# An attention state stored without its zero blocks, with the head pairs of odd batches swapped in PSUM

## The chip, the cores and the metric

The kernel runs on one core of a Trainium2 chip. The metric is the time of one execution on the device, in microseconds (us); lower is better.

## What is computed

A linear attention with a decaying state, then two feed-forward parts. The attention has 4 batches, 8 heads, 768 positions and head size 48:

```python
for t in range(S):
    cur = np.einsum('bhd,bhe->bhde', u[None] * kt, vt)
    y[:, :, t] = np.einsum('bhd,bhde->bhe', rt, state + cur)
    state = w[None, :, :, None] * state + np.einsum('bhd,bhe->bhde', kt, vt)
```

`y`, laid out as 3072 tokens by 384, goes into a soft mixture of experts (softmax of `x @ phi` over the tokens and over 32 slots, 8 experts with a hidden layer of 1024), and its result through a dense layer 384 to 2048 to 384 with a leaky ReLU. All of it is in fp32.

## The kernel before

The attention runs in chunks of 128 positions (`C`), 6 chunks of 4 head pairs: 24 **units**, unit `i` being chunk `c = i // 4` and pair `hp = i % 4`. A unit holds all 4 batches of its two heads. Head 0 of a pair lies on partitions 0 to 47, head 1 on 64 to 111; so a tile "of a pair" has 112 partitions (`R`).

For each unit TensorE (PE) runs these steps, in program order, with the names that the profile shows:

- `scores(i + 1)`: `A`, k against r, eight products of 48 rows, the two heads in two row tiles of the array, each head into a PSUM bank of its own.
- `attend(i)`: `y`, in two parts. The **state step** (line 392, from chunk 1 on): four products, one for each batch, `Sbd` (112 x 112, two 48 x 48 blocks on the diagonal and zeros elsewhere) against r. The **base step** (line 399): eight products of the masked scores `base` with v, the heads in two column tiles.
- `update(i)`: `U`, k against v for the next state, eight products of 48 columns.
- `logits(i - 1)`: `l`, `x @ phi`, four products of 32 weight columns, each batch in a column tile of its own.
- `tokens(i - 1)`: `px`, four transposes.

In the second unit of each chunk (`k == 1`) there are besides: `soft2`, which transposes two tiles of the chunk before (`pt`, which ScalarE copies to `dl` and `call`), and `slots` (`pS`, four products of 384 columns, the batches in four column tiles).

Around them GpSimd (POOL) scales r and forms the bonus product two units ahead (`scale`, `bonus`, `keys`); VectorE (DVE) scales k, puts the masked scores into `base` (`keep`, line 369), reduces the bonus to `Dg` (line 323), folds `U` into the state (line 422, one instruction for each head) and narrows a weight in eight of the units (`low`); ScalarE (ACT) writes `base` from `Dg` (line 338, eight instructions), copies `y` to `xT` (line 432) and `px` to `xtok`, and takes the exponentials of the softmax (`d`, line 483). The engines run their instructions in program order; no scheduler reorders them (`manual_schedule`). The line of all loads is SP's: in each unit a weight of 768 KB, and the r, k (512 KB) and v, k, r tokens (576 KB) of the unit four ahead, whose buffers (five of them) are freed by PE's last read.

PSUM has 8 banks: `A` two, `y` one, `ylast` one (it shares the tag of the powers `ETp`), `l` one, and three that rotate (`psM`) among `U`, `px`, `pS`, `pt` and `low`. The last unit writes two `y` tiles, so that ACT can copy the first half while PE makes the second.

After the attention come the expert layers (`ph`, `po`) and, from about 163 us on, 96 steps of the dense layer (`h`, and line 1005, `o`).

Of the kernel before, what the change touches and what calls it, by code (L numbers as in the profile page):

```python
# [8 lines left out]
F32 = mybir.dt.float32  # L9
# [4 lines left out]
ALU = mybir.AluOpType  # L14
AX = mybir.AxisListType
PSUM = bass.MemoryType.PSUM

B, H, S, D = 4, 8, 768, 48
C = 128
# [98 lines left out]
def chunked(ctx, tc, rk, tok, wT, urep, phi, w1, w2, win, wout, outT, dbg=None, check=False):  # L118
# [10 lines left out]
    phi_sb = cp.tile([R, NP, NS], F32, name="phi_sb")  # L129
# [69 lines left out]
    psM = att.enter_context(tc.tile_pool(name="psM", bufs=3, space=PSUM))  # L199
# [59 lines left out]
    warm = psY.tile([128, 512], F32, name="warm", tag="y")  # L259
# [3 lines left out]
    def warmup(n):  # L263
        for k in range(n):
            nc.tensor.matmul(warm, zz[:, 0:128], zz, start=True, stop=True)
# [24 lines left out]
    def powers_t(hp):  # L290
# [8 lines left out]
    Sbd = ap.tile([R, NP, B, R], F32, name="Sbd")  # L299
    nc.scalar.copy(  # L300
        Sbd.rearrange("p a b c -> p (a b c)"), zz[:R, 0:1].broadcast_to([R, NP * B * R])
    )
# [72 lines left out]
    yps, xT, xtok, lps, lw = {}, {}, {}, {}, {}  # L375

    def attend(i):
        c, hp = divmod(i, NP)
        y = yps[i] = psY.tile([128, B, C], F32, name=f"y{i}", tag="y")
        if i == NU - 1:  # L380
            ylast = psE.tile([128, B, C], F32, name="ylast", tag="E")
            yps[i] = y, ylast
        for _ in range(FILL.get(i + 1, 0)):
            nc.tensor.matmul(
                y.rearrange("p b t -> p (b t)"), zz[:, 0:128], zz, start=True, stop=True
            )
        v = tk_t[i][:, 0]
        for bs in (range(B),) if i < NU - 1 else (range(B // 2), range(B // 2, B)):
            if bs[0]:
                y = ylast  # L390
# [5 lines left out]
            for b in bs:  # L396
                for h in range(2):
                    n = 64 if c == 0 and h == 0 else D
                    nc.tensor.matmul(  # L399
                        y[64 * h : 64 * h + n, b, :], v[:, b, D * h : D * h + n],  # L400
                        base[i][:, h, b, :], start=c == 0, stop=True, skip_group_check=True,
                    )

    def update(i):
        c, hp = divmod(i, NP)
        if c < NC - 1:
            v = tk_t[i][:, 0]
            u = psM.tile([128, B, D], F32, name=f"U{i}", tag="m")
            kk = tk_t[i][:, 1]
            for b in range(B):  # L410
                for h in range(2):
                    nc.tensor.matmul(  # L412
                        u[64 * h : 64 * h + D, b, :], kk[:, b, D * h : D * h + D],
                        v[:, b, D * h : D * h + D], start=True, stop=True,
                    )
            for h in range(2):
                p = slice(64 * h, 64 * h + D)
                st = Sbd[p, hp, :, p]
                if c == 0:
                    nc.vector.tensor_copy(st, u[p])  # L420
                else:
                    nc.vector.scalar_tensor_tensor(  # L422
                        st, st, W128[p, hp : hp + 1], u[p], op0=ALU.mult, op1=ALU.add
                    )

    def evac(i):
        x = xT[i] = bp.tile([R, B, C], F32, name=f"xT{i}", tag="xT")
        if i == NU - 1:
            nc.scalar.copy(x[:, 0:2], yps[i][0][0:R, 0:2])
            nc.vector.tensor_copy(x[:, 2:4], yps[i][1][0:R, 2:4])  # L430
        else:
            nc.scalar.copy(x, yps[i][0:R])

    def logits(i):
        c, hp = divmod(i, NP)
        if hp == 0:
            lw[c] = psL.tile([128, 4, C], F32, name=f"l{c}", tag="l")
            lps[c] = lw[c][:, 0]
        for b in range(B):
            nc.tensor.matmul(  # L440
                lps[c][32 * b : 32 * b + 32, :], phi_sb[:, hp, :], xT[i][:, b, :],
                start=hp == 0, stop=hp == NP - 1, skip_group_check=True,
            )
# [57 lines left out]
    def soft2(c):  # L501
        pt = psM.tile([128, 2, 128], F32, name=f"pt{c}", tag="m")
# [7 lines left out]
    def slots(c):  # L510
        pS = psM.tile([128, DM], F32, name=f"pS{c}", tag="m")
        for b in range(B):
            nc.tensor.matmul(
                pS[32 * b : 32 * b + 32, :], dTs[c][:, 32 * b : 32 * b + 32], xtok[c][:, b, :],
                start=True, stop=True,
            )
        return pS
# [47 lines left out]
    for i in range(NU):  # L565
# [76 lines left out]
    pz = psM.tile([128, 512], F32, name="pz", tag="m")  # L642
    pt = psM.tile([128, 2, 128], F32, name="ptl", tag="m")
# [14 lines left out]
    pS = slots(NC - 1)  # L658
# [449 lines left out]
def _layout(i):  # L1108
# [27 lines left out]
    a["phi"] = ph.reshape(NP, 128, NS)[:, :R].transpose(1, 0, 2)  # L1136
# [42 lines left out]
```

## Time and profile before

| | us |
|---|---|
| median of 3 runs | 394.1 (393.93 to 395.03) |
| the profiled execution | 393.61 |
| its span, first to last instruction | 391.8 |
| the attention, to the last `y` product | 123.9 |

The granted TensorE clock is 1.00 (2.4 GHz) through the attention and 0.998 over the span. In the rows below a matmul of fp32 counts as two instructions (`x16` is eight products). The end of a matmul is modelled, and matmuls overlap: how long a step holds PE is read from its start to the start of the next step, not from its length.

### The profile page before, as it was taken

How to read it: one execution, taken by the hardware profiler on the slowest of the kernel's cores; microseconds unless marked ns; L12 is line 12 of the kernel's file. 1: busy time of each engine (PE TensorE's matmuls, PEld its weight loads, DVE VectorE, ACT ScalarE, POOL GpSimd, SP SyncE). 2: the span in 40 equal slices, each digit the busy share in tenths (PEclk: the TensorE clock that was granted, in tenths of full speed). 3: DMA queues.
4: the chain of work that ended last, by engine and by line, in shares of the span. 5: the costliest groups of instructions: out<-in, count | busy, mean ns of one | idle time of the engine just before them, and what ended most of it. 6: DMA issues, size and time to landing. Idle time of an engine off the chain costs nothing.

```text
span 391.8 us, 8004 instructions
## 1 busy us (share of the span) xinstructions
PE 375.6 (96%) x2978; PEld 289.9 (74%) x2978; DVE 278.8 (71%) x483; ACT 236.3 (60%) x551; POOL 149.9 (38%) x150
## 2 busy tenths in 40 slices
PE   6897999999999999899999999999999999999994
PEld 3566888887866343788888878888888888888883
DVE  6789898898973736757677764677866776586762
ACT  4377787878784215566676548667655445545540
POOL 4798999988630401145523332555200000000000
PEclk9999999999999999999999999999999999999999
DMA  7999999999997799500022220000000120021202
GB/s 255 413 419 414 413 416 417 416 418 416 408 364 255 280 390 416 215 0 0 2 81 81 82 80 2 1 0 3 1 1 2 54 106 2 2 109 53 80 1 88
DMA packets 21088, 70.07 MB, mean 179 GB/s; under 512 B 2240, under 2 KB 7344, under 8 KB 20912
## 3 DMA queue, kind: packets, MB, share of 16 engines
q1 hardware_dynamic: 21040, 69.47, 45.4%
q8 instruction: 25, 0.41, 0.4%
q14 instruction: 23, 0.19, 0.2%
HBM read 64.74 MB, written 4.72 MB: 177 GB/s over the span
## 4 chain that ended last, share of the span: by engine, by line
PE 78%; DVE 8%; POOL 5%; issue 4%; ACT 3%; POOLq 0%; DVEq 0%; ACTq 0%
PE o L1005 50%; PE h L948 6%; PE po L783 3%; PE ph L740 3%; PE y L392 3%; PE A L361 3%; PE y L399 2%; DVE base L369 2%; ACT base L338 2%; POOL rkb L309 2%; PE px L448 1%; DVE Dg L323 1%; PE U L412 1%; DVE Sbd L422 1%; PE l L440 1%
## 5 line engine op out<-in xcount | busy, mean ns | idle before, releaser
L962 ACT CAST gh<-t 128x512 fp32r<-128x512 f32 x94 | 58.4, 622 | 69.6 <-DVE t L958 66.6
L958 DVE TENSOR_TENSOR t<-t,h 128x512 f32<-128x512 f32 (+1 forms) x97 | 65.7, 678 | 25.0 <-ACT t L954 24.2
L1005 PE MATMUL o<-gh,wol 128*128 128x512 f32 x279 | 80.1, 393 | 0.0
L1005 PE MATMUL o<-gh,woh 128*128 128x512 f32 x279 | 80.0, 393 | 0.0
L1005 PE MATMUL o<-gl,woh 128*128 128x512 f32 x279 | 79.7, 392 | 0.0
L967 DVE TENSOR_TENSOR gl<-t,gh 128x512 fp32r<-128x512 f32 x71 | 50.3, 709 | 40.6 <-ACT gh L962 39.9
L954 ACT ACTIVATE t<-h 128x512 f32<-128x512 f32 (+1 forms) x97 | 57.4, 593 | 12.3 <-PE h L948 11.2
L1005 PEld LDWEIGHTS o<-gl,woh 128*128 128x128 f32 x279 | 52.4, 188 | 11.8
L1005 PEld LDWEIGHTS o<-gh,woh 128*128 128x128 f32 x279 | 52.4, 188 | 11.8 <-DVE sum L1076 0.2
L1005 PEld LDWEIGHTS o<-gh,wol 128*128 128x128 f32 x279 | 52.2, 188 | 11.8 <-issue 0.4
L338 ACT ACTIVATE base<-anti,Dg 128x128 f32<-128x128 f32 x176 | 53.9, 391 | 8.8 <-DVE Dg L323 8.8
L967 POOL TENSOR_TENSOR gl<-t,gh 128x512 fp32r<-128x512 f32 x23 | 34.3, 1491 | 51.0 <-ACT gh L962 43.1
L948 PE MATMUL h<-cT,Gs 128*128 128x512 f32 (+1 forms) x97 | 37.4, 391 | 1.4 <-ACT Gs L916 1.4
L369 DVE COPY_PREDICATED base<-mask,A 128x512 f32<-128x512 int32 x48 | 33.7, 733 | 4.1 <-ACT base L338 3.0
L361 PE MATMUL A<-rkb 48*128 48x128 f32 x384 | 28.2, 286 | 3.0 <-DVE base L369 1.3
L361 PEld LDWEIGHTS A<-rkb 48*128 48x128 f32 x384 | 23.8, 189 | 8.4 <-POOL rkb L309 2.8
L309 POOL TENSOR_TENSOR rkb<-rkb,ETw 112x512 f32<-112x512 f32 x23 | 27.5, 1198 | 4.1 <-DMA rkb<-in_rk_dram 3.9
L399 PE MATMUL y<-base,tk 128*48 128x128 f32 (+1 forms) x376 | 25.5, 277 | 0.0
L315 POOL TENSOR_TENSOR tk<-tk,u_sb 128x384 f32<-128x384 f32 x22 | 22.5, 1022 | 4.4 <-DMA tk<-in_tok_dram 2.4
L318 POOL TENSOR_TENSOR tk<-tk 128x384 f32<-128x384 f32 x22 | 22.3, 1012 | 1.7
L850 POOL TENSOR_TENSOR wol<-wor,woh 128x384 fp32r<-128x384 f32 x8 | 9.5, 1198 | 33.6 <-ACT woh L849 33.6
L399 PEld LDWEIGHTS y<-base,tk 128*48 128x48 f32 (+1 forms) x376 | 19.5, 124 | 3.7 <-issue 0.8
(200 smaller groups left out, 499.4 us busy)
## 6 DMA issues: line engine op xcount, KB each, us to landing
w<-in_w_dram SPq DMA_DIRECT2D x24, 768.0 KB, 9.8
tk<-in_tok_dram SPq DMA_DIRECT2D x23, 576.0 KB, 8.1
rkb<-in_rk_dram SPq DMA_DIRECT2D x24, 512.0 KB, 8.4
wir<-in_win_dram SPq DMA_DIRECT2D x8, 768.0 KB, 12.9
out_dram<-sum SPq DMA_DIRECT2D x17, 256.0 KB, 2.0
wor<-in_wout_dram SPq DMA_DIRECT2D x4, 768.0 KB, 8.4
wir<-in_wout_dram SPq DMA_DIRECT2D x4, 768.0 KB, 4.2
w2t<-in_w_dram SPq DMA_DIRECT2D x4, 576.0 KB, 5.7
```

What stands on the lines that cost most here:

```text
L309: (nc.vector if x else eng).tensor_tensor(t, t, e, op=ALU.mult)
L315: eng.tensor_tensor(rr, rr, u_sb[:, hp : hp + 1, :].broadcast_to([128, B, 2 * D]), op=ALU.mult)
L338: nc.scalar.activation(base[i][:, h, b, :], anti, AF.Copy, scale=Dg[i][:, h * B + b : h * B + b + 1])
L361: nc.tensor.matmul(a[:, h, b, :], rk_t[i][p0 : p0 + D, 1, b, :], rk_t[i][p0 : p0 + D, 0, b, :], start=True, stop=True,)
L369: nc.vector.copy_predicated(base[i][:, :, 2 * j : 2 * j + 2, :], mask.unsqueeze(1).unsqueeze(1).broadcast_to([128, 2, 2, C]), a[:, :, 2 * ...
L399: nc.tensor.matmul(y[64 * h : 64 * h + n, b, :], v[:, b, D * h : D * h + n], base[i][:, h, b, :], start=c == 0, stop=True, skip_group_chec ...
L948: nc.tensor.matmul(t, Gs[f // 8][:, f % 8 * 128 : f % 8 * 128 + 128], cT[blk // 3][:, blk % 3 * TB + c.start : blk % 3 * TB + c.stop], sta ...
L954: nc.scalar.mul(tt[n][:, c], t, 0.01)
L958: nc.vector.tensor_tensor(tt[n][:, c], tt[n][:, c], h, op=ALU.max)
L962: nc.scalar.copy(gh[n][:, c], tt[n][:, c])
L967: eng.tensor_tensor(gl[n][:, c], tt[n][:, c], gh[n][:, c].bitcast(F32), op=ALU.subtract)
L1005: nc.tensor.matmul(os[m][:, c], w[j][:, k, m * 128 : (m + 1) * 128], g[n][:, c], start=k == 0 and w is woh and g is gh and c.start == 0, s ...
```

## The change

`Sbd` becomes `St`, 112 partitions by 48 columns for each batch and pair, without the zero blocks; the copy that zeroed `Sbd` at the start goes away. The state step becomes eight products of 48 x 48. `y` becomes one tile `Y` of two banks for all units: the batch's parity `r` chooses the bank, its half `j` the place in it, and a head of parity `r` goes to partitions `64 * (h ^ r)`, so that in odd batches the two heads change places. Four products in a row then use the four quarters of the array (64 x 64 each). The base step follows the same places.

What reads `y` follows too: `phi` comes with a second copy with heads swapped (112 KB in place of 56), `slots` takes two products of 192 columns in place of one of 384 for odd batches, and `evac` copies from two banks. The new state is folded in by one DVE instruction of 112 partitions in place of two of 48; since it reads all 112, `U` of head 0 takes 64 weight columns in place of 48.

`Y` takes two banks: so `psM` keeps two buffers in place of three, and `ylast` is gone. `pt` moves from `psM` into the bank of `l`, so `logits` of a new chunk can begin only when `dl` and `call` are copied; `slots` is moved ahead of `logits`.

```diff
-    psM = att.enter_context(tc.tile_pool(name="psM", bufs=3, space=PSUM))
+    psM = att.enter_context(tc.tile_pool(name="psM", bufs=2, space=PSUM))
...
+    Y = psY.tile([128, 2, 4, C], F32, name="Y", tag="y")
...
-            for b in bs if c else ():
+        for j in range(B // 2) if c else ():
+            for r in range(2):
+                b = 2 * j + r
+                for h in range(2):
+                    g, p = 64 * (h ^ r), slice(64 * h, 64 * h + D)
+                    nc.tensor.matmul(
+                        Y[g : g + D, r, j, :], St[p, hp, b, :], rk_t[i][p, 0, b, :],
+                        start=j == 0, stop=False, skip_group_check=True,
+                    )
+        for j, r in ((0, 0), (0, 1), (1, 0), (1, 1)) if i < NU - 1 else ((0, 0), (1, 0), (0, 1), (1, 1)):
+            b = 2 * j + r
+            for h in range(2):
+                g = 64 * (h ^ r)
                 nc.tensor.matmul(
-                    y[0:R, b, :], Sbd[:, hp, b, :], rk_t[i][:, 0, b, :], start=b == bs[0],
-                    stop=False, skip_group_check=True,
+                    Y[g : g + D, r, j, :], v[:, b, D * h : D * h + D], base[i][:, h, b, :],
+                    start=c == 0, stop=True, skip_group_check=True,
                 )
...
+                    n = D if h else 64
                     nc.tensor.matmul(
-                        u[64 * h : 64 * h + D, b, :], kk[:, b, D * h : D * h + D],
+                        u[64 * h : 64 * h + n, b, :], kk[:, b, D * h : D * h + n],
...
-            for h in range(2):
-                p = slice(64 * h, 64 * h + D)
-                st = Sbd[p, hp, :, p]
...
+            st = St[:, hp]
...
-        pt = psM.tile([128, 2, 128], F32, name=f"pt{c}", tag="m")
+        pt = lw[c][:, 1:3]
...
+            p, x = slice(32 * b, 32 * b + 32), xtok[c][:, b, :]
+            for h in range(2) if b % 2 else (None,):
+                nc.tensor.matmul(
+                    pS[p] if h is None else heads(pS[p])[:, h], dTs[c][:, p],
+                    x if h is None else heads(x)[:, 1 - h], start=True, stop=True,
+                )
...
-        if i >= 1:
-            logits(i - 1)
         if c and k == 1:
             pS = slots(c - 1)
         if i >= 1:
+            logits(i - 1)
             tokens(i - 1)(nc.scalar.copy)
```

PE in unit 13 (the second of chunk 3) and at the start of unit 14, before; a row counts products:

```order
L412 MATMUL U_910<-tk_554 48x48 x8
L440 MATMUL l_921<-xT_813,phi_sb 32x128 x4
L513 MATMUL pS_926<-xtok_631,dl_895 32x384 x4
L448 MATMUL px_931<-ident,xT_813 128x112 x4
L361 MATMUL A_951<-rkb_110 128x128 x8
L392 MATMUL y_964<-rkb_109,Sbd 112x128 x4
L399 MATMUL y_964<-base_817,tk_640 48x128 x8
```

The same place of the changed kernel, from the last two products of `U` on:

```order
L410 MATMUL U_914<-tk_547 64x48
L410 MATMUL U_914<-tk_547 48x48
L516 MATMUL pS_924<-xtok_627,dl_899 32x384
L516 MATMUL pS_924<-xtok_627,dl_899 32x4x48 x2
L516 MATMUL pS_924<-xtok_627,dl_899 32x384
L516 MATMUL pS_924<-xtok_627,dl_899 32x4x48 x2
L437 MATMUL l_931<-xT_816,phi_sb 32x128 x4
L445 MATMUL px_936<-ident,xT_816 128x112 x4
L360 MATMUL A_956<-rkb_110 128x128 x8
L388 MATMUL Y<-rkb_109,St 48x128 x8
L396 MATMUL Y<-base_820,tk_636 48x128 x8
```

The state step went from four products to eight, `pS` from four to six, and `l` stands behind `pS`.

DVE in unit 13, before (`st` and `acc` belong to the softmax):

```order
L323 TENSOR_REDUCE Dg_898<-tk_709 128x4x2
L422 SCALAR_TENSOR_TENSOR Sbd<-Sbd,W_139,U_910 48x4x48 x2
L524 SCALAR_TENSOR_TENSOR acc<-acc,st_850,pS_926 128x384
L172 TENSOR_SCALAR low_940<-wir_272 128x384
L178 SCALAR_TENSOR_TENSOR low_940<-wi,low_940 128x384
```

And DVE there in the changed kernel:

```order
L322 TENSOR_REDUCE Dg_902<-tk_707 128x4x2
L418 SCALAR_TENSOR_TENSOR St<-St,W_139,U_914 112x192
L527 SCALAR_TENSOR_TENSOR acc<-acc,st_852,pS_924 128x384
L172 TENSOR_SCALAR low_945<-wir_269 128x384
L178 SCALAR_TENSOR_TENSOR low_945<-wi,low_945 128x384
```

One instruction stands where two stood; nothing else moved.

## Rows read from the trace of the kernel before

**Rows 1.** The page: PE's busy time and instructions; GB/s in 40 slices.

```profile
PE 375.6 (96%) x2978; PEld 289.9 (74%) x2978; DVE 278.8 (71%) x483; ACT 236.3 (60%) x551; POOL 149.9 (38%) x150
...
GB/s 255 413 419 414 413 416 417 416 418 416 408 364 255 280 390 416 215 0 0 2 81 81 82 80 2 1 0 3 1 1 2 54 106 2 2 109 53 80 1 88
```

**Rows 2.** Windows of four units each: length, busy by engine, clock, DMA share, GB/s.

```profile
41.57:60.65 19.08, 19.00 (x284) 15.50 (x283) 17.07 (x34) 15.37 (x50) 17.54 (x17) 1.00 1.02 416
...
79.72:98.79 19.07, 19.00 (x284) 15.49 (x284) 17.10 (x34) 15.65 (x51) 15.81 (x16) 1.00 1.02 417
```

**Rows 3.** Timeline of PE in unit 10: start, length, line, out<-in, count.

```profile
60.65 1.16 PE L361 MATMUL A<-rkb 48*128 48x128 f32 x16
61.74 1.13 PE L392 MATMUL y<-rkb,Sbd 112*112 112x128 f32 x8
62.80 1.08 PE L399 MATMUL y<-base,tk 128*48 128x128 f32 x16
63.71 0.53 PE L412 MATMUL U<-tk 128*48 128x48 f32 x16
64.16 0.43 PE L440 MATMUL l<-xT,phi_sb 112*32 112x128 f32 x8
64.52 0.60 PE L448 MATMUL px<-ident,xT 112*128 112x112 f32 x4
65.05 0.38 PE L361 MATMUL A<-rkb 48*128 48x128 f32 x2
```

**Rows 4.** Waits from 41.57 to 117.57 us: total, times, longest.

```profile
ACT xT L432 <- PE y L399: 11.2, 12, 2.1
...
PEld pt L503 <- ACT d L483: 1.1, 4, 0.5
```

**Rows 5.** The chain that ended last, units 7 to 9: start, length.

```profile
49.21 0.38 PE U L412 x16
...
49.62 0.40 DVE Sbd L422
...
52.82 1.36 DVE base L369 x2
54.18 0.44 DVE Dg L323
...
54.71 2.46 ACT base L338 x8
...
58.69 0.49 PE U L412 x16
...
59.54 0.65 PE pS L513 x8
```

**Rows 6.** Group of the state update from 41.57 to 117.57: busy us, mean ns | idle.

```profile
L422 DVE SCALAR_TENSOR_TENSOR Sbd<-Sbd,W,U 48x192 f32<-48x192 f32 x28 | 11.5, 411 | 3.2 <-PE U L412 2.6
```

**Rows 7.** Weight loads by shape from 11 to 45 us: 48 and 64 columns.

```profile
L399 PEld LDWEIGHTS y<-base,tk 128*48 128x48 f32 x80 | 5.8, 123 | 0.4
L399 PEld LDWEIGHTS y<-base,tk 128*64 128x64 f32 x32 | 3.4, 136 | 1.1 <-issue 0.8
```

**Rows 8.** Timeline of POOL, the last unit's data (unit 23).

```profile
108.30 1.28 POOL L309 TENSOR_TENSOR rkb<-rkb,ETw 112x512 f32<-112x512 f32 x1 [0.99 <-DMA rkb<-in_rk_dram]
...
110.94 1.00 POOL L318 TENSOR_TENSOR tk<-tk 128x384 f32<-128x384 f32 x1
```

**Rows 9.** Timeline of PE, the last unit, to the first `l` behind it.

```profile
121.52 0.65 PE L392 MATMUL y<-rkb,Sbd 112*112 112x128 f32 x4
...
123.87 0.32 PE L440 MATMUL l<-xT,phi_sb 112*32 112x128 f32 x4
```

**Rows 10.** Timeline of ACT and PE in units 11 and 12.

```profile
71.22 0.46 ACT L454 COPY xtok<-px 128x384 f32<-128x384 f32 x1
...
72.52 0.53 PE L412 MATMUL U<-tk 128*48 128x48 f32 x16
```

**Rows 11.** Window of the dense layer, columns as in Rows 2.

```profile
165.00:391.00 226.00, 221.20 (x996) 180.49 (x994) 150.96 (x222) 130.60 (x226) 48.77 (x37) 1.00 0.10 36
```

More of the change, by code (lines that the diff above doesn't have):

```diff
@@ L128, in chunked @@
     call = cp.tile([128, B, NC, NS], F32, name="call")
-    phi_sb = cp.tile([R, NP, NS], F32, name="phi_sb")
+    phi_sb = cp.tile([R, NP, 2, NS], F32, name="phi_sb")
     acc = cp.tile([128, DM], F32, name="acc")
@@ L264, in warmup @@
         for k in range(n):
-            nc.tensor.matmul(warm, zz[:, 0:128], zz, start=True, stop=True)
+            nc.tensor.matmul(
+                Y[:, k].rearrange("p a t -> p (a t)"), zz[:, 0:128], zz, start=True, stop=True
+            )
     ex = scr[:R, 512:1536].rearrange("p (n t) -> p n t", n=NP)
@@ L297, in powers_t @@
         )
[L299 to L302, printed above, removed]
+    St = ap.tile([R, NP, B, D], F32, name="St")
     def scale(i, eng=nc.gpsimd, part=(0, 1)):
@@ L373, in keep @@
             )
-    yps, xT, xtok, lps, lw = {}, {}, {}, {}, {}
+    xT, xtok, lps, lw = {}, {}, {}, {}
     def attend(i):
         c, hp = divmod(i, NP)
[L379 to L382, printed above, removed]
         for _ in range(FILL.get(i + 1, 0)):
             nc.tensor.matmul(
-                y.rearrange("p b t -> p (b t)"), zz[:, 0:128], zz, start=True, stop=True
+                Y[:, 0].rearrange("p a t -> p (a t)"), zz[:, 0:128], zz, start=True, stop=True
             )
         v = tk_t[i][:, 0]
-        for bs in (range(B),) if i < NU - 1 else (range(B // 2), range(B // 2, B)):
-            if bs[0]:
-                y = ylast
-            for b in bs if c else ():
+        for j in range(B // 2) if c else ():
[11 more added lines that the diff above has]
+                g = 64 * (h ^ r)
                 nc.tensor.matmul(
-                    y[0:R, b, :], Sbd[:, hp, b, :], rk_t[i][:, 0, b, :], start=b == bs[0],
-                    stop=False, skip_group_check=True,
-                )
-            for b in bs:
-                for h in range(2):
[L398 to L402, printed above, removed]
+                    Y[g : g + D, r, j, :], v[:, b, D * h : D * h + D], base[i][:, h, b, :],
+                    start=c == 0, stop=True, skip_group_check=True,
+                )
     def update(i):
@@ L508, in soft2, with heads, slots @@
         dTs[c] = dl
-    def slots(c):
-        pS = psM.tile([128, DM], F32, name=f"pS{c}", tag="m")
-        for b in range(B):
[L513 to L516, printed above, removed]
+    def heads(x):
+        return x.rearrange("p (n h d) -> p h n d", h=2, d=D)
+    def slots(c, pS=None):
+        if pS is None:
+            pS = psM.tile([128, DM], F32, name=f"pS{c}", tag="m")
+        for b in range(B):
+            p, x = slice(32 * b, 32 * b + 32), xtok[c][:, b, :]
+            for h in range(2) if b % 2 else (None,):
+                nc.tensor.matmul(
+                    pS[p] if h is None else heads(pS[p])[:, h], dTs[c][:, p],
+                    x if h is None else heads(x)[:, 1 - h], start=True, stop=True,
+                )
         return pS
@@ L640, in chunked @@
     tok_copy(nc.vector.tensor_copy)
-    pz = psM.tile([128, 512], F32, name="pz", tag="m")
-    pt = psM.tile([128, 2, 128], F32, name="ptl", tag="m")
+    yl = psY.tile([128, 2, 512], F32, name="yl", tag="y")
+    pz, pt = yl[:, 0], lw[NC - 1][:, 1:3]
     dl = sm.tile([128, 128], F32, name="dll", tag="dl")
@@ L657, in chunked @@
         )
-    pS = slots(NC - 1)
+    pS = slots(NC - 1, yl[:, 1, 0:DM])
     rescale(NC - 1)
@@ L1135, in _layout @@
     ph[:, :, :D] = np.asarray(i["moe_phi"]).reshape(NP, 2, D, NS)
-    a["phi"] = ph.reshape(NP, 128, NS)[:, :R].transpose(1, 0, 2)
+    ph = np.stack([ph, ph[:, ::-1]], 1).reshape(NP, 2, 128, NS)
+    a["phi"] = ph[:, :, :R].transpose(2, 0, 1, 3)
     a["w1"] = np.asarray(i["moe_w1"]).reshape(E, KT, 128, 2, FE // 2).transpose(0, 3, 2, 1, 4)
```

23 lines of the change are left out of this document (11 added, 12 removed).

## Prediction

> **What bounds the kernel now.** I read the page first [rows 1]: PE is busy for 96% of the span, so PE is asked first, stage by stage. The change touches the attention alone. Windows of four units each [rows 2] say that in each 19.08 us PE is busy 19.00; DVE follows with 17.07, POOL with 17.54, ACT with 15.37, and the DMA engines are full (share 1.02, 416 GB/s). So PE is the bound there, with two others close behind. The granted clock is 1.00 (2.4 GHz) in these windows; PE stays busy after the change, and nothing is put down to the clock.
>
> One unit on PE [rows 3], from start to start: `A` 1.09, the state step 1.06, the base step 0.91, `U` 0.45, `l` 0.36, `px` 0.53; 4.40 in all, with no idle time behind any of them. The state step is the second longest, and it is the only one whose instructions stand one behind another: its 8 take 1.06, where `A` and the base step put 16 of the same 128 columns into about the same time (two tiles of the array at once), and `l` puts 8 into 0.36 (four tiles at once).
>
> PE has one appointment in each chunk that it keeps late: `pt` in the second unit waits for the exponentials of ACT (1.1 us of its weight loads, in four chunks) [rows 4]. The chain of waits shows what lies ahead of that [rows 5]: `U` of unit 7 at 49.21, two state updates on DVE from 49.62, `low`, `keep` at 52.82, `Dg`, `base` on ACT from 54.71 to 57.17, the exponential, `pt`, and `U` of unit 9 on PE at 58.69. In that half of a chunk PE and the DVE-ACT chain are equally long; in the other half PE alone is the path. This decides how much of PE's saving reaches the end.
>
> **The change part by part.** *The state step.* Eight products in four tiles are 16 instructions in four rounds of four. No row shows four quarters of the array at once. The nearest: `l`, two rounds of four column tiles, 0.36; `A`, eight rounds of two row tiles, 1.09. The line between them gives (1.09 - 0.36) / 6 = 0.12 a round, so four rounds take 0.36 + 2 x 0.12 = 0.60 us and 1.06 - 0.60 = **0.46 us a unit** is saved. Bounds: half of the old step, 0.53 saved; or no two quarters more than the two tiles that `A` shows, eight rounds, 1.06, nothing saved. I take 0.46, since `l` runs four tiles, `A` two rows, and the quarters differ from both only in having rows and columns split together.
>
> The two heads of a batch write one PSUM bank, from different row tiles; in `A` the two row tiles write two banks, so no row shows that either, and the price if they can't is the rival below. The Trainium skill (TensorEngine Tiling (Array Packing), Restrictions and Gotchas, Gotcha 1) says that different row tiles write to different banks and can't access the same bank at the same time; by that the step would stay at 1.06. No run here shows it yet, and I read the rule as one on the same partitions of a bank, which the swap of the heads avoids; that is a reading, and it has its chance.
>
> *The base step* has as many products in pairs of column tiles as before: nothing. *`U`*: eight products, four of them with 64 weight columns. A load of 64 takes 136 ns where one of 48 takes 123 [rows 7]: 13 ns for each of the eight loads, at most +0.10; nothing, if the columns streamed bound it. I take +0.05. *`pS`*: for odd batches two products of 192 for one of 384. If the four tiles stay filled, nothing; if the second 192 holds up the batch behind it, half of the 0.65 of `pS` [rows 5] again, +0.32. A chunk has one; I take +0.15. `l` behind `pS` waits for `call`, which ACT writes while `U` and `pS` run: nothing, and 0.3 if that cover were gone.
>
> *DVE*: one instruction of 112 partitions for two of 48, 411 ns each [rows 6]; the elements of a partition (192) stay, so 0.41 a unit goes. *ACT*: `evac` copies as many elements from two banks; the zeroing at the start goes, beside which DVE works: nothing. *SP*: 56 KB more of `phi`, at 416 GB/s 0.14 us once, behind which the first loads queue; taken as nothing. `psM` with two buffers: costed as a rival.
>
> **The sum.** From `pt` of one chunk to `pt` of the next, on the path: PE from `pt` to the `U` two units later holds two state steps, three `U` and one `pS`: -2 x 0.46 + 3 x 0.05 + 0.15 = -0.62. Then the DVE-ACT chain: -0.41. Together -1.03 of 19.07. Between the first `pt` (39 us) and the last (115 us) lie four such rounds: -4.1. Behind the last `pt` PE alone is the path: one state step, -0.46, `pS` +0.15, and the last unit, which now takes 2.35 from its first product to `l` [rows 9], since it changes twice between its two kinds of products; with one change it takes 0.60 and, for the base step and the change behind it, some 1.0: -0.75. In all -4.1 - 1.06 = **-5.2 us**. Before the first `pt` the units wait for data and for DVE; I count nothing there.
>
> Can the data follow? The DMA engines are full, so loads won't land earlier, however early a buffer is freed. The last unit's k and r are scaled from 108.30, waiting 0.99 for DMA, and its bonus ends at 111.94 [rows 8]. Behind that `Dg` 0.44, `base` 2.46 and `keep` 1.36 [rows 5] and half of the base step, 0.45, must follow: 116.7. Now the last `y` ends at 123.87. So up to 7.2 us can be won before the loads become the bound, and 5.2 fits. The expert layers and the dense layer behind have PE busy 221.20 of 226.00 [rows 11] and only shift; the loads of the expert weights have room, since GB/s falls to 255 and 280 in the slices from 117 to 137 us [rows 1].
>
> The profiled execution takes 393.6, so it would take 388.4; the median of the runs is 394.1, 0.5 above: **388.9**.
>
> **The rivals.** *PE alone sets the pace*: the DVE-ACT chain has more room than the chain of waits shows, because its pieces start earlier as PE frees `A`. Then each round gives 4 x (0.46 - 0.05) - 0.15 = 1.49, four give 6.0, with the end 7.0, just inside the 7.2 of the loads: **387.1**. For it: ACT waited 11.2 us for `y` [rows 4]. Against: `pt` waits for ACT already.
>
> *ACT holds PE back at the two buffers.* With two buffers `U` of unit 12 takes the buffer of `px` of unit 10, which ACT copies to `xtok` at 71.22 to 71.68; `U` starts at 72.52 [rows 10], 0.84 of room. If ACT's half doesn't move, PE arrives 3 x 0.46 - 3 x 0.05 - 0.15 = 1.1 earlier and waits; what is queued behind it on PE is `l`, `px` and the next `A`, for which DVE's `keep` waits. A round then gives some 0.5, and the whole 4 x 0.5 + 1.06 = 3.1: **391.0**.
>
> *The four quarters take turns* (the change doesn't do what it says, and the kernel gets slower): the two row tiles in one bank go one after the other, and the state step stays 1.06. Then `U` and `pS` are added alone: a round costs +0.35 to +0.72, four rounds 1.4 to 2.9, the end -0.38 for the change saved and +0.15 to +0.32. With DVE's 0.41 idle beside PE that is +1.2 to +2.8: 395.3 to 396.9, **396.1**. It decides from where the state step saves less than 0.09 a unit. For it: no row shows rows and columns split at once. Against: each of the two alone overlaps fully.
>
> **How the numbers follow.** About 0.3% (1.2 us) is what a measurement can tell from no change: faster is under 392.9, slower over 395.3. Forecast (388 to 390) 0.45; PE alone 0.20; ACT holds 0.18; turns 0.12, nearly all of it slower; 0.05 for a mixture that cancels out. A third of the ACT case may lose more and fall to no change. Faster: 0.45 + 0.20 + 0.12 = 0.77; same 0.11; slower 0.12. The range takes in both neighbours and the bounds of the state step: with 0.53 a unit saved and `U` and `pS` free, the loads' limit of 7.2 holds, 386.9, and a little for earlier loads gives 386.3; above, the ACT case with `U` and `pS` at their dear ends, 391.0 + 4 x 0.4, gives 392.6. Outside lie the turns and a few hundredths more.
>
> **What would show it.** In the changed profile the state step, from its first start to the base step's, at 0.55 to 0.65 (1.06 would be the turns); the matmuls of four quarters starting within some ten ns of each other; four units in about 18.0 us, where 17.6 says PE alone and 18.6 ACT; `U` at 0.45 to 0.55 and `pS` at 0.65 to 0.97; one state update of about 0.41 on DVE; the last `y` at about 118.7; the dense layer as long as before. PE idle in front of `U` or `px` for `xtok` would be the two buffers. POOL's rows of the last unit should stay near 108: if they move later with PE, the loads were tied to it and the limit of 7.2 is wrong. A state step over 0.97 breaks the prediction.

## The result: slower by 0.8%

The changed kernel takes 397.1 us (median of 12 runs, 395.3 to 401.3) where the kernel before took 393.6 (12 runs, 392.8 to 395.0): ratio 1.0084, 95% interval 1.0069 to 1.0099. The forecast was 388.9, faster. Ratios leave out a kernel's runs that are over 1.5% above its fastest; medians and ranges are of all its runs. The profiled execution of after took 397.37 (span 395.6, mean granted clock 0.980), against 393.61 (391.8, 0.998) before; over its twelve runs the mean granted clock lies between 0.972 and 0.991. The parts that the prediction was about came out nearly as priced; the time was lost in two places that it had left out, and the rounds gave less than half of what it expected.

The same marks in both traces (us from the span's start) show where the 3.8 us came from:

| mark | before | after | difference |
|---|---|---|---|
| `A` of unit 6 starts | 35.64 | 36.77 | +1.13 |
| first `pt` | 39.13 | 40.33 | +1.20 |
| `pt` four rounds on | 115.14 | 114.68 | -0.46 |
| last `y` product starts | 123.67 | 121.99 | -1.68 |
| `pS` of the last chunk | 127.18 | 125.58 | -1.60 |
| first `ph` of the experts | 130.21 | 132.13 | +1.92 |
| `hp` behind it | 138.07 | 142.49 | +4.42 |
| first `o` of the dense layer | 163.59 | 168.01 | +4.42 |
| end | 391.76 | 395.61 | +3.85 |

So the start lost 1.2, the four rounds won 1.66, the end of the attention won another 1.2, the 17 us from the last `pS` to `hp` lost 6.0, and the dense layer won 0.6. The page of after shows the two lost places as dips of the clock's row, in the third and the fourteenth slice, and PE's share falls from 96% [rows 1] to 94:

```profile
span 395.6 us, 8340 instructions
PE 372.1 (94%) x3162; PEld 285.3 (72%) x3162; DVE 270.2 (68%) x463; ACT 234.8 (59%) x550; POOL 148.8 (38%) x150
PEclk9989999999999599999999999999999999999998
```

**The rounds.** Windows from one `pt` to the next, with the columns of [rows 2]:

```profile
58.88:77.49 18.61, 17.39 (x318) 14.02 (x319) 15.39 (x29) 15.59 (x51) 17.44 (x18) 1.00 1.02 417
77.49:96.09 18.60, 17.40 (x319) 14.03 (x319) 15.39 (x29) 15.59 (x51) 16.02 (x16) 1.00 1.02 414
```

PE's work fell from 19.00 to 17.40 a round, but the round only from 19.07 to 18.60: PE is idle for 1.2 us in each. Its timeline in units 8 and 9, to be held against [rows 3], shows where:

```profile
58.88 0.33 PE L500 MATMUL l<-ident,d 128*128 128x128 f32 x1 [1.16 <-ACT lsb L487]
59.04 0.27 PE L501 MATMUL l<-ident,lsb 128*128 128x128 f32 x1
59.24 0.67 PE L410 MATMUL U<-tk 128*64 128x48 f32 x16
59.84 0.86 PE L516 MATMUL pS<-xtok,dl 128*32 128x384 f32 x12
60.51 0.41 PE L437 MATMUL l<-xT,phi_sb 112*32 112x128 f32 x8
...
62.48 0.66 PE L388 MATMUL Y<-rkb,St 48*48 48x128 f32 x16
63.06 1.08 PE L396 MATMUL Y<-base,tk 128*48 128x128 f32 x16
63.97 0.61 PE L410 MATMUL U<-tk 128*64 128x48 f32 x16
64.52 0.32 PE L437 MATMUL l<-xT,phi_sb 112*32 112x128 f32 x4
```

The state step takes 0.58 (62.48 to 63.06); its instructions start in fours, the first four within 20 ns (62.477 to 62.497), the next four from 62.625. `U` takes 0.55, `pS` 0.67; the idle time stands in front of `pt` (its first line here, under the name of `l`, whose tile it now shares), which waits for ACT. It waits for `lsb`, which reads `l` in that tile; `d`, which it needs itself, ends 0.43 us earlier (58.39 against 58.82). The waits of the four rounds, which [rows 4] gave for before, say that ACT and DVE wait for one another as well:

```profile
ACT base L337 <- DVE Dg L322: 6.3, 8, 0.9
...
DVE base L368 <- ACT base L337: 5.5, 13, 0.4
PE l L500 <- ACT lsb L487: 5.4, 5, 1.2
```

**The end of the attention.** The timelines of after behind the last `pS`, first PE, then ACT, DVE and POOL. (In after `pS` of the last chunk lies in the tile `yl`, beside the maxima that were `pz` before; the section on the change does not tell this.)

```profile
125.58 0.87 PE L516 MATMUL yl<-xtok,dll 128*32 128x384 f32 x12
128.74 0.69 PE L679 MATMUL pZ<-selb,ones 128*128 128x64 f32 x2 [2.28 <-DVE cb L673]
...
132.13 10.43 PE L742 MATMUL ph<-w,slT 128*32 128x512 f32 x72
```

```profile
126.54 0.26 ACT L662 ACTIVATE cb<-yl,mst 128x1 f32<-128x1 f32 x1 [0.81 <-PE yl L516]
```

```profile
126.83 1.85 DVE L667 TENSOR_SCALAR selb<-Q,cb,sst 128x64 f32<-128x64 f32 x1 [0.85 <-ACT cb L662]
127.06 1.66 DVE L667 TENSOR_SCALAR selb<-Q,cb,st 128x64 f32<-128x64 f32 x1
```

```profile
126.61 2.02 POOL L711 MEMSET hTm<- 128x2304 f32 x1 [14.78 <-PE yl L516]
```

`cb` reads only the maxima, but here the wait for the tile covers all that was written to it, so it waits for `pS`; before, `cb` ran at 127.22, while `pS` was running. That makes `selb` late, and then it takes 1.85 and 1.66 us where it took 0.31 each before: both end at 128.7, with POOL's clearing of `hTm` (126.61 to 128.63). PE has nothing to do for 2.28 us, and then runs at half the clock (1.2 GHz) for the next ten:

```profile
127.00:137.40 10.40, 8.66 (x43) 4.48 (x47) 6.77 (x13) 1.82 (x5) 3.71 (x10) 0.51 0.41 144
```

From `ph` to `hp` then takes 10.36, where it took 7.86.

**The start.** PE's rows of unit 1, and ACT's beside them:

```profile
19.16 0.43 PE L437 MATMUL l<-xT,phi_sb 112*32 112x128 f32 x8
21.28 1.01 PE L445 MATMUL px<-ident,xT 112*128 112x112 f32 x4 [1.69 <-ACT KH L296]
22.08 2.70 PE L580 MATMUL l<-u_sb,ident 128*128 128x384 f32 x4
```

```profile
18.18 2.45 ACT L337 ACTIVATE base<-anti,Dg 128x128 f32<-128x128 f32 x8 [1.22 <-DVE Dg L322]
20.53 0.56 ACT L429 COPY xT<-Y 112x512 f32<-112x512 f32 x1
21.00 0.23 ACT L296 COPY KH<-psE 128x96 f32<-128x96 f32 x1
```

With two `psM` buffers `px` of unit 0 takes the one that ACT must first copy to `KH`, and that copy stands behind 2.45 us of `base`. The filler product behind it then takes 2.70 where it took 1.47, at half the clock.

The fall of the clock does not follow from the program alone. Seven traced kernels (with those below) have this start and a wait of 1.32 to 1.70 us for `KH`; in four of them the clock fell behind it and in three it stayed at 1.00. In those three `A` of unit 6 starts at 35.67 to 36.10, so the wait by itself costs 0 to 0.5 us at this mark, and the rest of the 1.13 came with the clock.

### The profile page after: what moved, and what is told of

Its sections match the earlier page's. It is cut to its first block, busy times and chain, and to the rows that moved or that the text cites. A ratio compares the mean times of both kernels' runs of the same rounds, so it can differ in the third digit from the quotient of the medians.

```text
span 395.6 us, 8340 instructions
## 1 busy us (share of the span) xinstructions
PE 372.1 (94%) x3162; PEld 285.3 (72%) x3162; DVE 270.2 (68%) x463; ACT 234.8 (59%) x550; POOL 148.8 (38%) x150
## 4 chain that ended last, share of the span: by engine, by line
PE 73%; DVE 10%; ACT 10%; issue 3%; POOL 3%; POOLq 0%; DVEq 0%; ACTq 0%
PE o L1007 50%; ACT base L337 7%; PE h L950 6%; PE ph L742 3%; PE po L785 3%; DVE base L368 3%; DVE Dg L322 2%; DVE rkb L308 1%; PE A L360 1%; PE px L445 1%; PE pS L516 1%; POOL rkb L308 1%; PE Y L388 1%; PE Y L396 1%; PE U L410 1%
## 5 line engine op out<-in xcount | busy, mean ns | idle before, releaser
L396 PE MATMUL Y<-base,tk 128*48 128x128 f32 x384 | 25.9, 277 | 0.0
L396 PEld LDWEIGHTS Y<-base,tk 128*48 128x48 f32 x384 | 19.8, 122 | 4.8 <-issue 3.3
```

The costliest lines, as they stand in the source:

```text
L396: nc.tensor.matmul(Y[g : g + D, r, j, :], v[:, b, D * h : D * h + D], base[i][:, h, b, :], start=c == 0, stop=True, skip_group_check=True,)
```

## The experiments

Each time comes with the ratio to the kernel before on the same chip. Three causes are told apart: the tail, the pace of the rounds, the start.

### The tail

**`pS` of the last chunk back in a `psM` tile.**

```diff
-    pS = slots(NC - 1, yl[:, 1, 0:DM])
+    pS = slots(NC - 1)
```

> The changed kernel with one line undone: the last slots product goes to a psM buffer of its own again, so that pz and pS no longer share one tile. My theory: behind the attention the scalar cb waits for pS because both lie in one tile, DVE's selb then stands behind POOL's memset of hTm, PE idles 2.3 us and its clock halves for about 10 us. Without the shared tile cb starts before pS ends, selb takes 0.3 us each, the time from the last pS start to the first ph is 3.0 to 3.5 us in place of 6.55, ph takes 7.9 us in place of 10.4, the clock stays 1.00, and the kernel takes 390.5 to 391.5 us. Rival: the clock falls because the state step now does less work on PE; then the clock falls here too and the time stays at 395 or more.

392.4 us (389.9 to 395.2; 390.5 to 391.5 was expected), ratio 0.9973 (0.9943 to 1.0004), against 1.0084: one line is worth 1.1%. `selb` comes ahead of POOL's clearing, not under it:

```profile
124.55 0.87 PE L516 MATMUL pS<-xtok,dll 128*32 128x384 f32 x12
125.42 0.43 PE L679 MATMUL pZ<-selb,ones 128*128 128x64 f32 x2
...
127.30 4.93 PE L742 MATMUL ph<-w,slT 128*32 128x512 f32 x44
```

```profile
125.05 0.32 DVE L667 TENSOR_SCALAR selb<-Q,cb,sst 128x64 f32<-128x64 f32 x1
125.28 0.31 DVE L667 TENSOR_SCALAR selb<-Q,cb,st 128x64 f32<-128x64 f32 x1
```

```profile
125.57 2.02 POOL L711 MEMSET hTm<- 128x2304 f32 x1 [13.51 <-PE pS L516]
```

From `pS` to `ph` it is 2.75 us (6.55 in after), and the clock stays at 1.00.

**POOL's clearing held back, the shared tile kept**, twice: behind a copy into a new tile of four bytes, and behind one into an unused column of `cb`.

```diff
+    held = cp.tile([128, 1], F32, name="held")
+    nc.gpsimd.tensor_copy(held, slT[:, KT - 1, 0:1])
     hTm = ep.tile([128, FT, E * (NS + SPE)], F32, name="hTm")
```

> The changed kernel with the shared tile kept and POOL's memset of hTm held back until slT is written. My theory (DVE's two selb instructions wait for POOL's memset): selb takes 0.3 us each in place of 1.85 and 1.66, the first matmul behind (pZ) starts about 1.3 us earlier, PE idles 1.0 us in place of 2.3, the clock stays, and the time is 391.5 to 392.5. If DVE was slow for another cause: selb stays over 1.5 us and the time at 397. If an idle time of 1 us is enough to lose the clock: 395.5 to 396.

```diff
+    nc.gpsimd.tensor_copy(cb[:, 6:7], slT[:, KT - 1, 0:1])
     hTm = ep.tile([128, FT, E * (NS + SPE)], F32, name="hTm")
```

> The kernel after with the clearing of hTm on GpSimd held back until the slots are scaled, as in the earlier run of that kind, but by a copy into an unused column of the tile cb instead of a new tile of four bytes. That earlier run had its tail back (ph 3.7 us sooner, o 6.2 us sooner), and its dense layer took 230.8 us where after has 227.6, so its time stood at 397.0. Theory one (the new tile moved the addresses of what lies behind it in SBUF and made the dense layer slower): the dense layer takes 227.5 to 228.2 here, the time is 390 to 392. Theory two (the later clearing itself, or what it moves, costs the dense layer): dense 230 to 231, time 396 to 397.5.

In both `cb` still waits 0.8 us for `pS`, but `selb` takes 0.32 and 0.31, and `pZ` starts 1.62 behind `pS` (after 3.16, before 0.87). So of the 2.29 us that after lost here 0.75 is the shared tile and 1.54 the clearing. The Trainium skill (SBUF — State Buffer, Who interferes with whom) says that DVE's `tensor_scalar` can take a port pair that it shares with GpSimd, and that whoever comes second is blocked until the first is done; the trace agrees, since both `selb` end with the clearing, and the two runs without the overlap show the short times.

From the first `pt` to `pZ` PE's marks in the two traces agree within 0.02 us, and behind it they do not: with the new tile the clock stayed, with the column of `cb` it fell. The windows from 126.5 to 128.5, first with the new tile, then with the column:

```profile
126.50:128.50 2.00, 1.93 (x19) 1.81 (x22) 1.40 (x7) 0.58 (x3) 0.00 (x0) 1.00 0.88 243
```

```profile
126.50:128.50 2.00, 1.93 (x11) 1.94 (x12) 1.11 (x5) 0.57 (x3) 0.00 (x0) 0.68 0.95 297
```

`hp` starts at 136.32 in the one and 139.59 in the other. The medians are 397.0 (ratio 1.0095, 1.0053 to 1.0137; 391.5 to 392.5 was expected) and 396.1 (0.9985, 0.9948 to 1.0021; its ten runs lie between 390.3 and 398.2, and the medians alone give 1.0047). The traces are of executions of 394.5 and 396.9. The first lost its gain in the dense layer, which took 230.8 us (after 227.6). Of the two theories put down for that neither held as it stood: without the new tile it took 229.6, between the two numbers that they gave, and a part of that is clock too (0.68 from 165 to 170 us). The cause stays open.

**PE kept busy under the wait**, with three products of 384 columns behind `pS`.

```diff
+    fl = psE.tile([128, DM], F32, name="fl", tag="E")
+    for _ in range(3):
+        nc.tensor.matmul(
+            fl, ident, u_sb.rearrange("p a d -> p (a d)"), start=True, stop=True
+        )
     rescale(NC - 1)
```

> The changed kernel with three products of 384 columns, whose result nobody reads, put on PE behind the last pS, in the idle time ahead of pZ; shared tile and memset as they are. My theory: cb, selb and pZ start as in the changed kernel (pZ some 3.2 us behind the start of pS), but the clock stays at 1.00, so pZ to ph take 1.7 us in place of 3.4 and ph 7.9 in place of 10.4: 392.8 to 393.6 us. If the clock falls for a cause other than PE's idle time: 397 or more.

395.0 us, ratio 1.0029 (1.0000 to 1.0058); 392.8 to 393.6 was expected. `pZ` comes no sooner (3.15 behind `pS`), but the clock stays at 1.00: `pZ` to `ph` takes 1.82 (after 3.39) and `ph` to `hp` 7.87 (10.36). So between these two traces 2.5 us of `ph` and 1.6 in front of it are the price of the clock alone, and the wait itself costs the rest. That price is not the same each time: in two other traced kernels with the same 3.2 us from `pS` to `pZ` (more work on PE, and the two copies on DVE, both below) `ph` to `hp` takes 8.93 and 9.34.

### What sets the pace of the rounds

**More work on PE**: the state step a second time in each odd unit from chunk 1 on, into a part of `Y` that nobody reads (`y` of this kernel isn't the reference's; only its times are used).

> The changed kernel with the state step done twice in odd units from unit 5 on (the second time into a part of Y that nobody reads): 0.58 us of PE work more in ten units, two of them in each round of four. If ACT and DVE set the pace of the attention (base, keep, Dg in a ring), PE takes it out of its idle time before pt, 1.2 us a round: the last y ends at 122.5 to 123.5 in place of 122.2. If PE is on the path: 1.2 us a round more, the last y at 127 to 128.

```profile
63.02:81.61 18.59, 18.20 (x350) 14.87 (x350) 15.39 (x30) 15.68 (x51) 17.11 (x17) 1.00 1.02 415
81.61:100.22 18.61, 18.21 (x350) 14.88 (x351) 15.41 (x30) 15.72 (x51) 17.05 (x18) 1.00 1.02 414
```

PE has 0.8 us more to do in a round and the round stays at 18.60; the wait in front of `pt` falls from 1.2 to 0.4. So PE's own work is not what sets the pace. (This one run took 401.7: its start lost 4.6 us more than after's, at half the clock. So its last `y` starts at 126.6, outside the 122.5 to 123.5 that was expected; from the first `pt` on that is 82.1 us, against 81.7 in after.)

**Less waiting between ACT and DVE**, with PE's work as it is. In the first unit of each round DVE sums `Dg` of two units on ahead of the masked copies instead of behind them, and `lsb`, of which `pt` waits for the copy, goes ahead of the exponential `d`. It is built on a kernel with the tail mended and a transpose at the start moved into `Y` (below).

```diff
+        early = c and k in EARLY and i + 2 < NU
+        if early:
+            bonus(i + 2)
+            reduce(i + 2)
         if i + 1 < NU:
             scores(i + 1)
             keep(i + 1)
-        if i + 2 < NU:
+        if i + 2 < NU and not early:
             bonus(i + 2)
...
+        if c < NC - 1:
+            nc.scalar.copy(lsb, l)
         if c == 0:
             nc.scalar.activation(d, l, AF.Exp, bias=st[:, 1:2], accum_out=sst[:, 0:1])
...
-        if c < NC - 1:
-            nc.scalar.copy(lsb, l)
```

> The previous kernel, and two pieces moved on the engines beside TensorE, with the same work on TensorE: in the first unit of each round Dg of two units on is reduced on DVE ahead of the masked copies (keep) instead of behind them, so that ACT's base of that unit does not wait 0.7 us for it; and the copy lsb of the logits goes ahead of d's Exp on ACT, so that pt's first transpose waits for d alone and not for four ACT instructions of about 0.1 to 0.2 us each behind it. Theory (rounds are set by the ring of ACT and DVE: base, keep, Dg, base, and d to pt): PE's wait ahead of pt falls from 1.2 us to 0.3 to 0.7, the round from 18.6 us to 17.8 to 18.2, last y at 118 to 119.5, time 1.5 to 3 us below the previous kernel (387 to 389.5). Rival (POOL's chain, 4.1 us a unit of bonus, keys and rescaling, or the landing of the loads sets the round): pt's wait shrinks, but another takes its place (DVE Dg or POOL's tk behind a DMA), the round stays 18.5 to 18.6 and the time is that of the previous kernel within 0.5 us. Second rival (TensorE's own work sets it): no change at all.

```profile
61.25:79.25 18.00, 17.36 (x321) 14.05 (x319) 15.26 (x30) 15.49 (x50) 17.17 (x18) 1.00 1.02 418
79.25:97.10 17.85, 17.35 (x321) 14.05 (x319) 15.27 (x30) 15.49 (x50) 16.41 (x16) 1.00 1.02 415
```

The round falls to 17.8 to 18.0 with the same 17.35 on PE, and `pt` no longer waits. 391.9 us, ratio 0.9935 (0.9911 to 0.9958), 2.6 us under the same kernel without these two moves (1.5 to 3 was expected, and 387 to 389.5 for the time). That the ring of ACT and DVE sets the pace is shown by these two runs. What each of the two moves is worth is not: `lsb` ended 0.43 us behind `d`, and `base` waited 0.72 us for `Dg`. The last kernel below has `lsb` ahead in every round and `Dg` early in two; in the two others `pt` still waits 1.47 and 0.89 us for `d`, but POOL is late there too.

In the trace of after the ring from one `pt` to the next (77.49 to 96.09) is this: PE to `pS` (79.4); DVE without a gap (`acc`, the narrowing, k's scaling, `keep`, `Dg`) to 84.2; `base` on ACT to 86.7; `keep`, `Dg`, `St`, the narrowing, the scaling, `keep` and `Dg` on DVE to 92.4; `base`, then `xtok`, `d` and the rest to `lsb` on ACT to 96.0. So it holds more of DVE than `keep` and `Dg`, and about 2 us of PE.

### The start

**The wait moved, not removed.** The transpose whose copy `px` waits for goes into a free part of `Y`, with the tail mended.

```diff
-        ps = psM.tile([128, 128], F32, name=f"psE{hp}", tag="m")
+        ps = Y[:, 1, 3] if hp == 2 else psM.tile([128, 128], F32, name=f"psE{hp}", tag="m")
```

> The kernel after with the last slot sums back in a tile of psM, and with the transpose of the third head pair's powers (the third of four at the start) put into a part of Y that is free there, instead of a psM tile, so that psM's two buffers don't make px of unit 0 wait for the copy of KH. Theory (the start's loss is the wait of px 0 for KH, 1.69 us in the trace of after, and the lower clock that follows it): A of unit 6 starts at 35.5 to 35.9 us, where after has 36.8, with the clock 1.00 from 20 us on; all later marks as in the run with the tail alone: rounds 18.6, last y's product near 121, 2.7 us from the last pS to the first ph plus 0.0 to 0.3; time 390.0 to 391.5 and a smaller spread than with the tail alone (389.9 to 395.2). Rival (the low clock at the start comes from something else, such as the second U's wait): unit 6 at 36.5 or later in the profile, and a time like the tail alone, 392.4 with the same spread.

394.5 us, ratio 1.0012 (0.9996 to 1.0028), worse than the tail alone. 390.0 to 391.5 was expected. Unit 6 starts at 39.12. The tile `Y` is read by `xT`, so the transpose waits for that copy, which is also behind `base`:

```profile
21.19 0.45 PE L295 MATMUL Y<-ident,scr 112*128 112x112 f32 x1 [3.22 <-ACT xT L429]
```

It is the mistake of the tail again: a free place in a tile that others use.

**The two copies on DVE**, ahead of the masked copies of unit 2, everything else as in after.

```diff
+        elif i == 1:
+            nc.vector.tensor_copy(xv, Y[0:R, :, 0:2])
...
-            powers_t(i + 1)
+            powers_t(i + 1, nc.vector.tensor_copy if i == 1 else nc.scalar.copy)
+            if i == 1:
+                keep(i + 1)
```

> The kernel after with one change at the start: in unit 1 the copy of xT and the copy of KH for the third head pair run on DVE, ahead of the masked copies of base 2, instead of on ACT behind 2.45 us of base 2. Theory (px of unit 0 waits for KH, KH for ACT, and the lower clock at 21 us follows that wait): px of unit 0 starts near 20 instead of 21.3, with the clock at 1.00 there; A of unit 6 near 35 to 35.6 instead of 36.8; rounds 18.6 and the tail as in after; time 395.3 to 396.3, 1 to 1.7 us under after's 397.1. Rival (DVE is the engine that waits next at the start, so that the masked copies of base 2 come later by the two copies, 0.8 us): unit 6 at 36.3 or later, time 396.6 to 397.6.

```profile
19.92 0.60 PE L447 MATMUL px<-ident,xT 112*128 112x112 f32 x4 [0.23 <-DVE KH L296]
20.36 1.47 PE L582 MATMUL l<-u_sb,ident 128*128 128x384 f32 x4
```

Unit 6 starts at 34.67 (after 36.77, before 35.64) with the clock at 1.00, earlier than was expected (35 to 35.6). 395.4 us, ratio 1.0060 (1.0037 to 1.0084). That is 1.7 us under after's median, but the kernel before was slower beside it too (394.3, beside after 393.6): by the ratios it is 0.9 us, and the intervals overlap (after 1.0069 to 1.0099). The trace shows the wait gone; that the whole time falls is not clear of noise.

**The kernel before with two `psM` buffers.**

```diff
-    psM = att.enter_context(tc.tile_pool(name="psM", bufs=3, space=PSUM))
+    psM = att.enter_context(tc.tile_pool(name="psM", bufs=2, space=PSUM))
```

> The kernel before with two psM buffers instead of three and nothing else. It prices the buffer that the change gave to Y. Theory (the third buffer only served the start, where px of unit 0 waits for KH's copy, and the tail): A of unit 6 1.0 to 1.3 us later than 35.6, rounds 19.05 to 19.15 as before, time +0.8 to +1.5 us against before. Rival (two buffers also bind in the rounds, by U, pS, px and the narrowing's tiles): rounds 19.3 or more, time +2 us or more. Rival (no price): within 0.3 us.

395.4 us, ratio 1.0038 (1.0020 to 1.0057): by the medians the buffer costs 1.2 us. The size was expected, the place was not: `px` waits 1.44 for `KH`, but the clock stays and unit 6 starts at 35.53; the four rounds take 76.94 where they took 76.01, 0.70 of it in the first. The profiled execution is the slowest of the ten (399.3): in it the clock fell behind the attention too (`ph` to `hp` 10.10), though `pZ` follows `pS` by 0.87 as in the kernel before.

### Together

The line of the tail and the two moves of the rounds:

> After with the tail's slot sums back in psM and with Dg ahead of keep in the first unit of each round and lsb ahead of d; the start as in after (without the transpose into Y that the run of both had, which made the start wait 3.2 us for xT). Theory: start as in after (unit 6 at 35.7 to 37), rounds 17.8 to 17.9 as in the run with the same two pieces, last y at 118 to 119, ph 2.7 us behind the last pS, time 388.5 to 390, that is 2 to 3.5 us under the same run with that start and about 3 us under the run with the tail alone (392.4). Rival (what the rounds gain is given back at the end, by loads that land no earlier): last y at 118 to 119 but the dense layer starts no more than 1 us sooner than in the run with the tail alone, time 391.5 to 392.5.

Those, and the two copies on DVE at the start:

> The two others of this set together: tail, rounds and start. Theory (three separate causes whose sizes add): unit 6 at 35 to 35.6, rounds 17.8 to 17.9, last y at 117 to 118, ph 2.7 us behind the last pS, time 387 to 389, 1.4% under before. Rival (the start's gain is lost, since the first rounds wait for the loads of rk and tok, which land in a fixed order at a fixed rate): last y as in the run of rounds and tail, time the same within 0.5 us.

And the same with `Dg` early in two rounds only:

```diff
-        early = c and k in EARLY and i + 2 < NU
+        early = c in (2, 3) and k in EARLY
```

> The kernel with tail, rounds and start together, with Dg ahead of keep only in the rounds that begin with units 8 and 12. In the run with all rounds A waited behind that order for 1.35 us ahead of unit 6 (with half the clock behind it), 1.17 at 91.9 and 1.55 at 110.3, since GpSimd had not finished the products that Dg sums. Theory (those waits are what ate the start's gain): unit 6 at 34.6 to 34.9 with the clock at 1.00, rounds 17.8 twice and 18.2 to 18.6 else, last y at 118.5 to 120, time 389 to 391. Rival (the last rounds are held by the landing of rk's loads, at 100, 104.5 and 109 us, whatever comes ahead): last y at 120 to 121, time 391 to 392, as the run with all rounds.

The marks of these (rounds from `pt` to `pt`; `ph` from its start to `hp`). The marks are of the profiled executions, which took 390.1 (tail), 394.1 (start), 391.0, 391.7 and 390.1 us (the last three lines):

| kernel | unit 6 | four rounds | last `pt` | last `y` | `ph` | median, ratio |
|---|---|---|---|---|---|---|
| before | 35.64 | 18.82 19.08 19.06 19.05 | 115.14 | 123.67 | 7.86 | 1 |
| after | 36.77 | 18.55 18.61 18.60 18.59 | 114.68 | 121.99 | 10.36 | 397.1, 1.0084 |
| tail | 35.67 | 18.53 18.61 18.60 18.59 | 113.64 | 120.95 | 7.86 | 392.4, 0.9973 |
| start | 34.67 | 18.54 18.60 18.84 18.57 | 112.86 | 120.17 | 9.34 | 395.4, 1.0060 |
| tail, rounds | 38.09 | 17.78 17.85 18.30 18.07 | 112.78 | 120.28 | 7.86 | 391.7, 0.9934 |
| tail, rounds, start | 36.17 | 17.77 17.86 18.52 19.31 | 113.87 | 121.67 | 7.86 | 391.5, 0.9940 |
| the same, `Dg` early in two rounds | 35.26 | 18.84 18.11 18.95 18.27 | 113.08 | 120.51 | 7.87 | 389.5, 0.9886 |

The three gains don't add: the first two of these kernels missed what was expected of them (388.5 to 390, and 387 to 389) and took the times that their rivals gave, though not with the marks of either. Who comes early into the rounds gets longer rounds, and the last `y` starts at 120.2 to 121.7 in each of the mended kernels. Two things stand behind that. `Dg` ahead of `keep` waits for POOL's product, and where POOL is late, `A` on PE waits behind it: 1.35 us ahead of unit 6 with all three, and the clock halved behind it (with tail and rounds alone 1.19, on top of a start that had lost the clock: 38.09). And the data: in the kernel with all three, POOL's last units wait for DMA, at a pace of 4.5 us a unit:

```profile
100.18 1.09 POOL L309 TENSOR_TENSOR rkb<-rkb,ETw 112x512 f32<-112x512 f32 x1 [0.99 <-DMA rkb<-in_rk_dram]
...
104.72 1.09 POOL L309 TENSOR_TENSOR rkb<-rkb,ETw 112x512 f32<-112x512 f32 x1 [1.00 <-DMA rkb<-in_rk_dram]
...
109.23 1.27 POOL L309 TENSOR_TENSOR rkb<-rkb,ETw 112x512 f32<-112x512 f32 x1 [1.00 <-DMA rkb<-in_rk_dram]
```

Four times that is 18.1 us: about what a round can cost at the least once the five buffers' lead is used up. Bytes give the same as an estimate: 1856 KB of loads a unit at 416 GB/s [rows 2] are 4.6 us, 18.3 a round. And POOL starts on the last unit's r and k at 108.25 to 111.1 in all fourteen traces, never sooner, whatever PE saved ahead of it. That this and not POOL's lateness is the floor was not tried apart. With `Dg` early only in the rounds of units 8 and 12 and the clock at 1.00 throughout the attention, the last kernel takes 389.5 us (388.3 to 390.5), ratio 0.9886 (0.9861 to 0.9912): below the kernel with all three (0.9917 to 0.9963), and its interval just meets that of tail and rounds (0.9909 to 0.9960). The time was expected (389 to 391), the marks were not: its rounds (74.2 together) are no shorter than after's (74.4), so what it wins over after lies in the start and the tail; its expected 17.8 came in neither of the two rounds, in each of which `A` waits for `keep` (1.51 and 0.75 us).

## Why the prediction was wrong, by its steps

- **The state step** was forecast at 0.60 and takes 0.58; four quarters do run at once (four starts within 20 ns), with the two heads of a batch in one bank on different partitions. That rival (0.12) is out. The rule of the Trainium skill (TensorEngine Tiling (Array Packing), Restrictions and Gotchas, Gotcha 1) that row tiles can't use one bank at the same time would have made it 1.06; the measurement decides against it for different partitions.
- **`U`, `pS`, the state update**: 0.55 (0.50 forecast), 0.67 (0.80 forecast, so nothing was added) and one instruction of 0.41: right.
- **The round, -1.03 forecast, -0.47 measured.** This step failed. From the chain [rows 5] it read that PE alone is the path in half of a round, and counted -0.62 there and -0.41 in the other half, for DVE's state update. PE was only the longer of two in its half. From `U` of unit 13 to `U` of unit 15 PE did become 0.75 faster (8.75, before 9.50), but the state update behind it starts 9.91 after `U` of unit 13 where it started 10.08 after it (77.86 and 77.68): the term of -0.62 gave -0.17, since DVE now stands in `keep` and `Dg` there:

```profile
86.61 0.61 PE L410 MATMUL U<-tk 128*64 128x48 f32 x16
...
87.32 0.55 DVE L322 TENSOR_REDUCE Dg<-tk 128x8 f32<-128x384 f32 x1
87.77 0.42 DVE L418 SCALAR_TENSOR_TENSOR St<-St,W,U 112x192 f32<-112x192 f32 x1
```

The other half, from there to `U` of unit 17, went from 8.99 to 8.68. PE collects the rest of its saving as a wait in front of `pt`. The wait for `pt` [rows 4] was already on the page and told that ACT was near; what was missing was the time of the ring by itself, from ACT's and DVE's rows. The rival "ACT holds PE back" gave the right size, 18.6 and some 0.5 a round, with the wrong reason: PE doesn't wait for `xtok` in front of `U` or `px` in the rounds. "PE alone" (17.6) came only close, at 17.8, once the ring was opened.

- **The end behind the last `pt`, -1.06 forecast**: from the last `pt` to the last `y` it is 7.31 against 8.53, -1.22; the last unit takes 1.59 to `l`, where 1.60 was forecast: right.
- **The start, "I count nothing"**: +1.2 in this execution, from a wait of 1.69 us for the second of two buffers and the clock that fell behind it; where the clock stayed, the same wait cost 0 to 0.5 at unit 6. The prediction priced the two buffers in the rounds, where they bind little, and not in the unit where the powers use them too.
- **"The expert layers and the dense layer only shift"**: this cost the sign. `pS` of the last chunk had moved into the tile of the maxima; the text speaks of `pS` only for its columns. A wait of 0.8 us pushed `selb` under POOL's clearing, the clearing made 2.3 us of idle PE, and the clock made 4 more in this execution. That the time came out near the 396.1 of the turns is chance. "Nothing is put down to the clock" was true of [rows 2], not of the places where PE runs dry.
- **The loads**: POOL's rows of the last unit stayed (108.33 against 108.30 [rows 8]), as forecast. The limit of 7.2 us was not reached: no mended kernel's last `y` started before 120.2, 3.5 us less than before. It followed the last unit from its landing and not the pace of landings; that this is why is argued, not shown.

## What to carry to other kernels

When PE is 96% busy, work taken from it is worth only the distance to the next ring: add up that ring from the rows of the other engines, and look for the wait (here `Dg` behind `keep`) that closes it. Putting a result into the free part of a tile joins its waits to those of all others in that tile: follow who reads that tile before the move, at the start and the end of a stage too. Behind a new gap on PE price the clock as well, as a range: here a gap of 2.3 us cost 1.6 to 4 us more in three traces.

## What the runs showed that was not expected

- Two kernels whose PE rows are alike from the first `pt` to 126.57 us went on, one at clock 1.00 and one at half of it: the same gap of PE ended either way. The runs of the second lie between 390.3 and 398.2; that this is the clock was not followed in each. The start shows the same (three of seven kept the clock), and the kernel before with two `psM` buffers lost it behind the attention though `pZ` follows `pS` as closely as before.
- A DVE instruction of 0.31 us took 1.85 beside a clearing on GpSimd, and was short again when either was moved by about 2 us.
- The dense layer, which no kernel here touches, has a pace of its own in each: a hundred `o` instructions take 25.31 us in after, 25.53 in before, 25.60 with the start mended, 25.83 with the new tile (from the starts in the traces, at clock 1.00). That is up to 2%; the whole layer took 227.6 to 230.8 us from its first `o` to the end. It is not the chip alone: two kernels that ran on different chips (the tail alone, and the transpose in `Y`) both have 25.31. The cause stayed open.
